# A one-core recurrence, Fourier mixing and MLP kernel: where the MLP pieces go, and what is kept in fixed order

## The chip, the core and the metric

The kernel runs on one core of a Trainium2 chip. The metric is the device time of one execution in microseconds (us). Before the change it is 781.95 us, the median of three runs (781.27 to 782.10); the profiled execution spans 780.2 us, and all times inside the trace are counted from its start.

## The reference, cut to what matters

Four batches, eight heads, 768 time steps, head size 48. First a delta-rule recurrence with a 48 x 48 state per batch and head, then, on its output put together to 768 x 384 per batch, a Fourier mixing, a normalisation and a two-layer MLP.

```python
# attention block: q, k, v are (4, 8, 768, 48), beta is (4, 8, 768)
k_n = k / (norm(k) + 1e-6)
for t in range(768):
    y[:, :, t] = einsum('bhd,bhde->bhe', q[:, :, t], state)
    v_old = einsum('bhde,bhd->bhe', state, k_n[:, :, t])
    state = state + beta_t * einsum('bhd,bhe->bhde', k_n[:, :, t], v[:, :, t] - v_old)

# x is y as (4, 768, 384)
mixed = real(fft(fft(x, axis=1), axis=2))
u  = x + mixed
un = (u - mean(u)) / sqrt(var(u) + 1e-6)                 # over the 384
out = u + maximum(un @ w_ch1, 0) @ w_ch2                  # 384 -> 1536 -> 384
```

The two weights arrive in 64-bit floating point and are turned into 32-bit on the core.

## The kernel before

**The recurrence in chunks.** Time is cut into chunks of 64 steps, 12 to a batch, so the chain has 48 steps m = 0 to 47. Each step needs the state of the step before it. It has three sections, each a group of small matmuls and then one operation of VectorE or ScalarE:

```python
def chain(m):
    ...                                   # pk = state x keys
    dve.tensor_tensor(U, V4[:, c], pk, op=ALU.subtract)      # section 0
    yield
    ...                                   # pu = wt x U
    act.activation(U, pu, ACT.Copy)                          # section 1
    yield
    ...                                   # pS = keys x U
    dve.tensor_tensor(nst, st, pS, op=ALU.add)               # section 2: the new state
    if n % 2 == 1:
        later.append(outputs(b, n, *pair))                   # y of two chunks, done later
    if c == QT - 1:
        scaled(Q + 1)                                        # V of the next four chunks x lengths
    yield
```

Four chunks make a quad Q, two quads a group g. Before its steps can run, a group needs `ahead(g)`: the keys and queries are transposed and their Gram matrices copied out of the matmul's memory (`prepare`), a triangular system is inverted on VectorE in 30 dependent rounds (`invert`), and the halves are put together by small matmuls and copies (`merge`). Groups 0 and 1 are prepared before the first chain step or during the first batch's steps.

```python
def gram_out(Q, c2, dst, src):
    if Q < 6 and c2:
        dve.tensor_copy(dst, src)
    else:
        act.activation(dst, src, ACT.Copy)

def invert(*gs):                          # per round j
    dve.tensor_tensor(t, X[:, :, j:j + 1, j + 1:], X[:, :, 0:j, j:j + 1], op=ALU.mult)
    dve.tensor_tensor(X[:, :, 0:j, j + 1:], X[:, :, 0:j, j + 1:], t, op=ALU.add)
    yield
```

**The mixing and the MLP.** When the chain of a batch has ended and its outputs are written to `x`, `fourier(b)` mixes it: sums and differences of halves on VectorE (`folded`, `shifted`), matmuls `pf` and `pb` with tables, additions back into `x`, and the statistics of the normalisation. For batch 0 the sums are made tile by tile (T = 2, 1, 0), since the last tile needs the last outputs. `mlps()` then works through the pairs of 128-row tiles, three pairs to a batch. Between two of its `yield`s lies a **piece**: mostly six matmul instructions `ph` (first layer) with one ScalarE operation, or four matmul instructions `po` (second layer).

**How they are laced together.** Python generators are advanced in turn. `beside()` advances the mixing of the last batch by one step, if there is one, and the MLP by one piece. `PRE` and `SIDE[b]` are the numbers of `ahead` steps and of pieces per section of a chain step, for the batch b whose chain is running.

```python
PRE, SIDE = 2.4, (0.0, 1.5, 2.2, 1.8)
pre, due, started = ahead(2), [0.0, 0.0], False
for m in range(NCH, STEPS):               # m = 12 .. 47
    b, n = divmod(m, NCH)
    g, Q = m // (2 * QT), m // QT
    count = 0
    while Q not in merged:                # the quad's merge is not traced yet
        advance(pre)
        count += 1
        if count % 3 == 0 and b > 1 or count % 4 == 0 and len(converted) == KF:
            beside()
    if m % (2 * QT) == 1:
        run(pre)
        pre = ahead(g + 1) if g + 1 < NG else iter(())
        due = [0.0, 0.0]
    for i, _ in enumerate(chain(m)):
        if i < 2:
            advancing(later)
        if n == 0 and i == 1:
            run(*later)
            later.clear()
            if b == 1:
                while advance(first_mixing):
                    if (0, 0) in norms or started:
                        started = advance(channels, 2)
            else:
                mixing[0] = fourier(b - 1)
        if b == 1 and (n > 0 or i > 1):
            advance(second, 3)            # second weight to 32 bit
        if m > NCH or i > 0:
            due[0] += 4.6 if g == 1 else PRE
            due[1] += SIDE[b]
        while max(due) >= 1.0:
            ...                           # beside() and advance(pre), one per unit due
run(*later)
mixing[0] = fourier(B - 1)
while beside() or mixing[0] is not None:
    pass
```

**Order.** The order of instructions on each engine is settled when the program is built: a scheduler may move an instruction ahead of others traced before it. While `strict[0]` is true, each TensorE, ScalarE and VectorE instruction is tied behind the one traced before it on its engine. That holds for the first batch's chain (m = 0 to 11) and a few places after it. What is traced later without this tie may still be moved in between.

```python
for m in range(1, NCH):                   # m = 1 .. 11, strict
    for i, _ in enumerate(chain(m)):
        ...                               # outputs, Gram matrices, merges at fixed places
        advance(next_keys, key_work.get((m, i), 0))
        if i == 1:
            ...
            elif m == 8:
                run(masks(2))
                advance(rest, 1)
            else:
                advance(rest, 5)          # first weight to 32 bit, then masks(3)
        if i == 2:
            advance(rest, 1)
            ...
            if m in (10, 11):
                advance(first_mixing)     # tiles 2 and 1 of the first mixing's sums
run(rest)
second = second_weight()
advance(second)
strict[0] = False
```

Of the kernel before, what the change touches and what calls it, by code (L numbers as in the profile page):

```python
# [82 lines left out]
def kernel(  # L83
# [15 lines left out]
    NCH = S // CH  # L99
# [3 lines left out]
    KF = DFF // 128  # L103
# [119 lines left out]
    def scaled(Q):  # L223

        if Q in vals and Q in lengths:
            vf = vals[Q].rearrange("p c u d -> p (c u) d")
            ln = lengths.pop(Q)
            dve.tensor_tensor(vf, vf, ln[:, :, None].broadcast_to([128, QT * 4, D]), op=ALU.mult)
# [129 lines left out]
    def second_weight():  # L358
        if moe_w_ch1.dtype == F32:
            yield  # L360
            nc.sync.dma_start(out=w2, in_=moe_w_ch2.rearrange("(c p) m -> p c m", p=128))
            converted.update(range(KF))
            return
        w2v = moe_w_ch2.bitcast(I32).rearrange("(c p) (m two) -> p c m two", p=128, two=2)

        stages = [xpairs[i].rearrange("p t (f two) -> p (t f) two", two=2).bitcast(I32) for i in (4, 5, 6)]

        def fetched(p):
            if p < KF:
                nc.sync.dma_start(out=stages[p % 3], in_=w2v[:, p])  # L370

        for p in range(3):
            fetched(p)
        yield
        digits(stages[0], *words(stages[0]))
        for p in range(KF):
            if p + 1 < KF:
                digits(stages[(p + 1) % 3], *words(stages[(p + 1) % 3]))
            ops = joined(w2[:, p], *words(stages[p % 3]))
            ops[0]()  # L380
            yield
            ops[1]()
            ops[2]()
            fetched(p + 3)
            converted.add(p)
            yield
# [3 lines left out]
    grams = {}  # L390

    def gram_out(Q, c2, dst, src):
        if Q < 6 and c2:
            dve.tensor_copy(dst, src)
        else:
            act.activation(dst, src, ACT.Copy)
# [8 lines left out]
    def masks(*Qs):  # L405

        for Q in Qs:
            for c2 in range(QT // 2):
                dst = ce(held[Q][2][:, 2 * c2:2 * c2 + 2])
                mask(Q, c2, dst, dst)  # L410
                yield

    def prepare(Q, parts=(0, 1)):
# [20 lines left out]
        for c2 in range(QT // 2):  # L434
# [29 lines left out]
            if 0 in parts:  # L464

                cj = slice(2 * QT * lh + 4 * c2, 2 * QT * lh + 4 * c2 + 4)
                Ae = A.rearrange("p l c (j e) s -> p e (c j) l s", e=2)[:, :, cj]
                for e in range(2):
                    gram_out(Q, c2, Ae[:, e], pv[:, e, :, 0, None, 0:W].broadcast_to([128, 4, 2, W]))
                for hh in range(2):  # L470
                    pr = slice(64 * hh + W, 64 * hh + 64)
                    gram_out(Q, c2, Ae[pr, :, :, 0], pv[pr, :, :, 0, W:])
# [172 lines left out]
    later = []  # L645
# [108 lines left out]
    def advancing(gens):  # L754

        if gens and next(gens[0], "end") == "end":
            gens.pop(0)
# [140 lines left out]
    done, converted = set(), set()  # L898
# [69 lines left out]
    def advance(gen, n=1):  # L968
        for _ in range(n):
            if next(gen, "end") == "end":  # L970
                return False
        return True

    def run(*gens):
        for gen in gens:
            for _ in gen:
                pass

    def seq(*gens):
        for gen in gens:  # L980
            yield from gen
# [74 lines left out]
    rest = seq(w.join(), masks(3))  # L1056
    first_mixing = fourier(0)
    for m in range(1, NCH):
        if m == 3:
            merges.update({2: Merge(1, 0, crossed=False), 3: Merge(1, 1, crossed=False)})  # L1060
        for i, _ in enumerate(chain(m)):
            if pe_work[m][i]:
                pe_work[m][i]()
            if m == 2 and i > 0:
                outs()
            if (m, i) in act_work:
                act_work[m, i]()
            advance(next_keys, key_work.get((m, i), 0))
            if i == 1:
                if m == 1:  # L1070
                    run(masks(0))
                    advance(first)
                elif m == 2:
                    scaled(1)
                    advance(first)
                elif m == 3:
                    run(masks(1))
                elif m == 6:
                    scaled(2)
                    advance(rest, 2)  # L1080
                elif m == 8:
                    run(masks(2))
                    advance(rest, 1)
                else:
                    advance(rest, 5)
            if i == 2:
                advance(rest, 1)
                if m in (3, 7):
                    w.split(10 + m // 7)
                if m in (10, 11):  # L1090
                    advance(first_mixing)
    run(rest)
    second = second_weight()
    advance(second)

# [12 lines left out]
    def ahead(g):  # L1108
        if g == 2:
            yield from kept(queries(4, 5))  # L1110
        for Q in (2 * g, 2 * g + 1):
            while Q >= NB and Q - NB in held and g > 2:
                yield
            if g > 2:
                yield from prepare(Q)
        yield from invert(g)
        for _ in merge(g):
            yield
# [4 lines left out]
    def beside():  # L1123

        if mixing[0] is not None:
            if not advance(mixing[0]):
                mixing[0] = None
        return advance(channels)


    PRE, SIDE = 2.4, (0.0, 1.5, 2.2, 1.8)
    pre, due, started = ahead(2), [0.0, 0.0], False
    for m in range(NCH, STEPS):
        b, n = divmod(m, NCH)
        g, Q = m // (2 * QT), m // QT

        count = 0
        while Q not in merged:
            advance(pre)
            count += 1  # L1140
            if count % 3 == 0 and b > 1 or count % 4 == 0 and len(converted) == KF:
                beside()
        if m % (2 * QT) == 1:
            run(pre)
# [15 lines that stand above are left out]
                advance(second, 3)  # L1160
# [4 lines that stand above are left out]
                if due[1] >= 1.0:  # L1165
                    due[1] -= 1.0
                    beside()
                if due[0] >= 1.0:
                    due[0] -= 1.0
                    advance(pre)  # L1170
# [34 lines left out]
```

## Time and profile before

| what | value |
|---|---|
| time, median of 3 | 781.95 us |
| profiled span | 780.2 us |
| TensorE (matmul) busy | 685.0 us, 88% |
| VectorE busy | 394.6 us, 51% |
| ScalarE busy | 258.1 us, 33% |
| GpSimd busy | 83.9 us, 11% |
| mean granted TensorE clock | 0.971 of full speed |
| mean DMA rate | 39 GB/s |

PE is TensorE's matmuls and PEld its weight loads, DVE is VectorE, ACT ScalarE, POOL GpSimd. Busy shares are means over parts of the program with different limits, so they say little about any one part; the table of stretches, which gives each engine's busy time, the granted clock and the DMA share between two given times, says more. The timeline of single instructions shows when one group of matmuls or one copy ran, and for how long.

The chain's sections can be found by their ScalarE operation `U<-pc`: step 0 at 89.8 us, step 12 (second batch) at 155.2, step 24 at 327.4, step 36 at 503.8, step 47 at 629.4. The last 100 us hold nothing but MLP.

### The profile page before, as it was taken

Reading aid. Unit: us, or ns where it says so; the run is one execution under the profiler, and the core shown is the slowest. Engines: PE = TensorE matmul, PEld = TensorE weight load, DVE = VectorE, ACT = ScalarE, POOL = GpSimd, SP = SyncE. Lnnn points to the kernel's source line nnn. Section 1 sums busy time; section 2 is a strip of 40 time slices with the busy share of each in tenths; the row PEclk is TensorE's granted clock in tenths of the full one; section 3 lists DMA queues with packets and bytes.
Section 4 is the critical chain, followed back from the end, with each engine's and each line's share of the span. In section 5 each row is a group of like instructions: output and inputs, shape, how many; then the busy total and the mean of one; then the engine's idle time right before and its main releaser. Section 6 shows DMA issues by size and latency. Waiting matters only on the chain.

```text
span 780.2 us, 18288 instructions
## 1 busy us (share of the span) xinstructions
PE 685.0 (88%) x7768; PEld 491.6 (63%) x7768; DVE 394.6 (51%) x980; ACT 258.1 (33%) x700; POOL 83.9 (11%) x116
## 2 busy tenths in 40 slices
PE   5943588869989998999899999878999989899996
PEld 4522577757747756567667577466667567577683
DVE  2599775977991399246595112887511125300000
ACT  3741355442335503535303444021623022021120
POOL 8010033323000000001100000011000000100000
PEclk9999999987999999999999999998999999999999
DMA  8642032341221211002201110100100000000000
GB/s 183 163 108 45 8 86 60 87 139 46 39 45 27 48 36 30 14 21 42 42 16 27 32 26 7 32 11 1 22 22 2 12 11 1 20 1 21 10 11 20
DMA packets 81041, 30.78 MB, mean 39 GB/s; under 512 B 75856, under 2 KB 77392, under 8 KB 80960
## 3 DMA queue, kind: packets, MB, share of 16 engines
q1 hardware_dynamic: 76560, 21.92, 13.2%
q0 software_dynamic: 2224, 7.31, 2.9%
q8 instruction: 61, 1.00, 0.5%
q10 hardware_dynamic: 2176, 0.39, 0.3%
q14 instruction: 20, 0.16, 0.1%
HBM read 24.87 MB, written 4.72 MB: 38 GB/s over the span
## 4 chain that ended last, share of the span: by engine, by line
PE 54%; DVE 26%; ACT 6%; SPq 5%; DMA 4%; issue 3%; POOL 1%; POOLq 0%; DVEq 0%; ACTq 0%
PE ph L131 20%; PE po L131 16%; DVE A L131 6%; DVE X L131 5%; PE pc L131 4%; SPq L219 4%; DVE x L131 3%; PE pf L131 3%; DVE w L131 3%; PE pj L131 2%; PE pb L131 2%; ACT A L131 2%; DMA qp<-in_q_dram 2%; ACT wt L131 2%; PE pg L131 2%
## 5 line engine op out<-in xcount | busy, mean ns | idle before, releaser
L131 PE MATMUL ph<-unT,w 128*128 128x256 f32 x864 | 212.1, 394 | 5.4 <-ACT hT L131 3.7
L131 PE MATMUL po<-w,hT 128*128 128x384 f32 x576 | 209.6, 508 | 0.0
L131 PEld LDWEIGHTS ph<-unT,w 128*128 128x128 f32 x864 | 159.8, 193 | 34.4 <-ACT hT L131 8.2
L131 PEld LDWEIGHTS po<-w,hT 128*128 128x128 f32 x576 | 105.6, 193 | 63.9 <-issue 4.9
L131 ACT ACTIVATE hT<-ph 128x256 f32<-128x256 f32 x144 | 55.0, 382 | 186.7 <-PE ph L131 186.3
L131 DVE TENSOR_TENSOR x<-x,po 128x384 f32<-128x384 f32 x24 | 13.2, 549 | 107.5 <-PE po L131 107.5
L131 PE MATMUL pg<-KQT 48*64 48x64 f32 (+1 forms) x1152 | 44.4, 297 | 5.8 <-ACT KQT L131 4.3
L131 ACT ACTIVATE U<-pc 128x192 f32<-128x192 f32 x48 | 15.8, 330 | 96.4 <-PE pc L131 82.7
L131 PEld LDWEIGHTS pg<-KQT 48*64 48x64 f32 x1152 | 34.0, 178 | 21.0 <-ACT KQT L131 11.0
L770 POOL DMA_INDIRECT out_dram<-x,rows_hi x12 | 12.3, 1025 | 321.1 <-DVE x L131 198.3
L131 DVE TENSOR_TENSOR U<-V,pc 128x192 f32<-128x192 f32 x48 | 16.7, 348 | 54.3 <-PE pc L131 54.3
L131 DVE TENSOR_TENSOR X<-X,A 128x30 f32<-128x30 f32 (+14 forms) x120 | 41.3, 344 | 3.0
L131 ACT ACTIVATE KQT<-pt 128x256 f32<-128x256 f32 (+1 forms) x84 | 33.0, 413 | 28.3 <-PE pt L131 26.9
L131 DVE TENSOR_TENSOR A<-X 128x30 f32<-128x30 f32 (+14 forms) x120 | 40.7, 339 | 3.0
L131 DVE TENSOR_TENSOR x<-x,pb 128x191 f32<-128x191 f32 (+1 forms) x72 | 24.9, 414 | 21.7 <-PE pb L131 21.7
L131 DVE TENSOR_TENSOR st<-st,pc 128x192 f32<-128x192 f32 x44 | 15.4, 350 | 40.2 <-PE pc L131 33.2
L131 PEld LDWEIGHTS pc<-U,wt 64*64 64x64 f32 x768 | 19.4, 156 | 24.2 <-DVE U L131 10.8
L131 PEld LDWEIGHTS pc<-st,KQT 48*64 48x64 f32 x768 | 18.6, 155 | 24.8 <-DVE st L131 11.9
L131 ACT ACTIVATE A<-pj 32x128 f32<-32x128 f32 (+1 forms) x76 | 20.7, 273 | 39.2 <-PE pj L131 38.4
L131 PE MATMUL pt<-pack,qp 128*128 128x128 f32 x96 | 22.4, 331 | 12.3 <-DMA qp<-in_q_dram 11.7
L131 PE MATMUL pc<-U,wt 64*64 64x48 f32 x768 | 25.8, 251 | 8.0 <-DVE U L131 6.2
L131 PE MATMUL pc<-st,KQT 48*64 48x48 f32 x768 | 25.3, 250 | 8.4 <-DVE st L131 8.1
(135 smaller groups left out, 855.3 us busy)
## 6 DMA issues: line engine op xcount, KB each, us to landing
x<-in_moe_w_ch_dram SPq DMA_DIRECT2D x14, 384.0 KB, 3.5
qp<-in_q_dram SPq DMA_DIRECT2D x96, 48.0 KB, 2.5
kp<-in_k_dram SPq DMA_DIRECT2D x80, 48.0 KB, 2.4
V<-in_v_dram SPq DMA_DIRECT2D x56, 48.0 KB, 2.3
w<-in_moe_w_ch_dram POOLq DMA_DIRECT2D x6, 384.0 KB, 8.2
x<-in_moe_w_ch_dram POOLq DMA_DIRECT2D x4, 384.0 KB, 7.7
V<-in_v_dram SPq DMA_DIRECT2D x64, 24.0 KB, 2.2
out_dram<-x SPq DMA_DIRECT2D x8, 192.0 KB, 1.9
```

Of the source, the lines that this page charges most:

```text
L131: ins = getattr(self.engine, name)(*args, **kwargs)
L219: eng.dma_start(out=vals[Q][64 * p:64 * p + CH, cs, u, :], in_=v[b, 4 * (p ^ (u % 2)) + u, t0:t0 + w * CH, :].rearrange("(c p) d -> p c d" ...
L770: nc.gpsimd.indirect_dma_start(out=out.rearrange("b s m -> (b s) m"), out_offset=bass.IndirectOffsetOnAxis(ap=rows_hi[:, i:i + 1], axis=0) ...
```

## The change

Five edits, none of which changes what is computed:

- the Gram matrices of quads 4 and 5 are copied out by ScalarE alone; before, VectorE took the second half of each;
- in step 11, the scaling of V for quad 3 is traced one section earlier, and at most three instead of five steps of the rest follow it;
- the last outputs of batch 0, and one more step of its mixing (sums of tile 0), are traced before the fixed order ends, so they keep their place;
- fewer MLP pieces beside the chain: 1.3 instead of 1.5 per section in batch 1, 2.0 instead of 2.2 in batch 2;
- more MLP pieces with the merges that a quad has to wait for: in batch 1 a piece after every step instead of every fourth, in the later batches after every second instead of every third or fourth.

The purpose is to have TensorE work at hand where it waits, and to have the first batch's end issued in the order in which its data become ready.

```diff
     def gram_out(Q, c2, dst, src):
-        if Q < 6 and c2:
+        if Q < 4 and c2:
             dve.tensor_copy(dst, src)
 ...
                 elif m == 8:
                     run(masks(2))
                     advance(rest, 1)
+                elif m == NCH - 1:
+                    scaled(3)
+                    advance(rest, 3)
                 else:
                     advance(rest, 5)
 ...
-    run(rest)
+    run(rest, *later)
+    later.clear()
+    advance(first_mixing)
     second = second_weight()
     advance(second)
 ...
-    PRE, SIDE = 2.4, (0.0, 1.5, 2.2, 1.8)
+    PRE, SIDE = 2.4, (0.0, 1.3, 2.0, 1.8)
 ...
             advance(pre)
             count += 1
-            if count % 3 == 0 and b > 1 or count % 4 == 0 and len(converted) == KF:
+            if len(converted) == KF and (b == 1 or count % 2 == 0):
                 beside()
```

## The prediction, made before the changed kernel was run

> **What bounds the kernel now.** I read the page's first two parts first, then a table of stretches, then single matmuls in the timeline. The page:
>
> ```profile
> PE 685.0 (88%) x7768; PEld 491.6 (63%) x7768; DVE 394.6 (51%) x980; ACT 258.1 (33%) x700; POOL 83.9 (11%) x116
> ...
> PE   5943588869989998999899999878999989899996
> DVE  2599775977991399246595112887511125300000
> ...
> PEclk9999999987999999999999999998999999999999
> ```
>
> TensorE is the busiest engine overall, and in the slices of 19.5 us it falls below 9 where VectorE rises to 7 to 9: in the first 200 us, and around 280, 390 and 490 to 550 us. So the bound changes from stretch to stretch. I cut the span at the ends of the inversions and mixings (columns: busy time and instructions of PE, PEld, DVE, ACT, POOL; granted clock; DMA share; GB/s):
>
> ```profile
> 104.00:152.00 48.00, 41.14 (x956) 34.75 (x956) 36.22 (x81) 26.20 (x69) 18.13 (x24) 1.00 0.36 86
> 152.00:176.00 24.00, 15.88 (x197) 13.75 (x196) 19.46 (x55) 10.05 (x22) 5.32 (x8) 0.85 0.41 120
> 176.00:236.00 60.00, 56.33 (x534) 38.56 (x533) 50.58 (x136) 19.29 (x55) 9.42 (x10) 0.90 0.19 42
> 236.00:270.00 34.00, 33.80 (x543) 26.20 (x542) 5.56 (x12) 20.16 (x58) 1.13 (x1) 0.98 0.19 37
> 270.00:312.00 42.00, 37.57 (x462) 24.46 (x454) 39.13 (x105) 9.07 (x25) 2.28 (x2) 1.00 0.18 36
> 312.00:378.00 66.00, 63.38 (x735) 44.80 (x736) 27.13 (x74) 30.07 (x86) 5.38 (x9) 1.00 0.14 28
> 378.00:420.00 42.00, 38.36 (x412) 25.61 (x411) 38.95 (x103) 9.68 (x27) 3.36 (x2) 1.00 0.12 27
> 420.00:484.00 64.00, 63.40 (x790) 45.00 (x790) 10.31 (x23) 28.63 (x88) 0.98 (x1) 1.00 0.11 23
> 484.00:556.00 72.00, 61.38 (x634) 43.20 (x625) 60.16 (x165) 17.60 (x45) 7.44 (x10) 0.91 0.08 18
> 556.00:636.00 80.00, 79.06 (x1008) 54.28 (x1008) 12.08 (x29) 21.52 (x65) 2.03 (x2) 1.00 0.03 12
> ```
>
> Length minus the first busy figure is TensorE's idle time: 6.9, 8.1, 3.7, 0.2, 4.4, 2.6, 3.6, 0.6, 10.6 and 0.9 us. Between them (236 to 270, 312 to 378, 420 to 484, 556 to 636, and the tail) TensorE has almost nothing to give. Its work is the same after the change, so the time can only fall where it stands still or runs slowly: above all 152 to 176 and 484 to 556, both mixings. What is missing in the second is seen if one asks for `po` alone:
>
> ```profile
> 322.00:367.00 45.00, 15.37 (x40) 6.79 (x40) 1.07 (x2) 1.00 0.12 26
> 498.70:543.70 45.00, 6.73 (x14) 3.08 (x14) 0.54 (x1) 0.85 0.04 12
> ```
>
> These are equal lengths from the first state of batch 2 and of batch 3, each holding a mixing. In the first TensorE does 40 `po` and 17 `ph` instructions beside it, in the second 14 and 32 (at the tail's pace of 0.325 and 0.216 us, 16.7 against 11.5 us of work). From 508.7 to 531 us there is no `po` and one `ph`: the MLP has used up batch 1 and waits for batch 2's statistics.
>
> The slow clock in that gap can be measured, too. One mixing matmul `pf` by one, from the timeline:
>
> ```profile
> 333.43 2.27 PE L131 MATMUL pf<-stab,scr 128*128 128x128 f32 x20
> 510.08 4.34 PE L131 MATMUL pf<-stab,scr 128*128 128x65 f32 x24 [2.38 <-DVE scr L131]
> ```
>
> 0.11 us each while MLP fills the gaps, 0.18 us each in the starved stretch.
>
> **What the Trainium skill says.** Its page "TensorE: Matmul & The Clock Gate", section "Part 1: The HAM clock gate (the "warmup" mystery)", says that TensorE's clock is halved after an idle window and freed again by sustained activity. The trace agrees in kind: the granted clock is 1.00 at 322 to 367 and 0.85 in the starved 498.7 to 543.7, and the `pf` above nearly double. It isn't consistent everywhere: from 40 to 80 us TensorE is mostly idle and the column still says 1.00. The page "Perfetto Trace Analysis", section "Engine Utilization", says that in a well-tuned kernel at least one engine approaches full utilisation; in the table above this holds except at 152 to 176, where VectorE has 19.5 of 24 us and TensorE 15.9.
>
> **The change part by part.**
>
> *Gram copies to ScalarE.* For each of quads 4 and 5, VectorE loses two copies of 128 x 256 (0.38 each) and two of 32 x 256 (0.43 each), as in
>
> ```profile
> 134.31 0.76 DVE L131 COPY A<-pg 128x256 f32<-128x256 f32 x2
> ...
> 135.96 0.86 DVE L131 COPY A<-pg 32x256 f32<-32x256 f32 x2
> ```
>
> 1.62 us a quad, 3.24 us in all. ScalarE gets them at the same kind of price (0.33 + 0.33 + 0.38 + 0.38 = 1.42 us, from its copies at 147.65 and 148.75), and is busy 26 of 48 us there. The first set sits before a merge matmul that waited 2.33 us for it; the second stands ahead of the sums of the mixing's tile 1 (153.47). Estimate on the path: 2 us of the 3.24.
>
> *Scaling of V in step 11.* Counting the advances, the rest's 36 + 2 steps are used up by step 10, so five or three makes no difference, and the scaling (0.95 us) already ran in step 11. 0 us.
>
> *Last outputs and tile 0 in order.* The y addition of the last outputs ran at 155.07, the first `pf` at 157.48; between them stand one section of chain step 12 and tile 0's sums. Nothing disappears, but conversion of the second weight and step 12 can no longer come in between so easily. The outputs' matmuls end at 153.0, ScalarE takes 0.49, the addition 0.55, the sums about 2: `pf` could start near 156. Estimate: 2 us with what the shorter wait saves behind it.
>
> *Pieces with the merges.* Batch 1, at step 16: by then 11 sections x 4.6 = 50 of the 58 steps that the first merged quad needs are done, so 8 are forced, and pieces with them go from 2 to 8. At 220 to 240 us TensorE is busy 17.0 of 20. Estimate: 2 of these 3 us. For batches 2 and 3 the old rule (every third or every fourth) hits 6 of 12 counts, the new one also 6 of 12: the rate is unchanged, 0 us.
>
> *Fewer pieces beside the chain.* Batch 1: 34 sections x 0.2 = 7 fewer, which the 6 above give back. Batch 2: 36 x 0.2 = 7 fewer, with nothing in return. A piece is 6 x 0.216 or 4 x 0.325 = 1.3 us, so 9.4 us of TensorE work leave the steps 24 to 35 and stay in store for the mixing of batch 2, which has 13 steps and takes a piece with each. The work isn't saved; it moves from where TensorE is full into the hole at 508.7 to 531, which has 6.3 us of idle time and a clock of 0.84 (0.16 x 22.3 = 3.6 us). From these 9.9 us I take 60%, as the mixing's own waits and VectorE (18.5 of 22.3 us busy) remain: 6 us. Against it, a third of the 7 pieces leave the inversions at 270 to 312 and 378 to 420, where VectorE sets the pace (39 of 42 us) and a missing piece becomes idle time: 7/3 x 1.3 = 3 us, of which some is refilled; I subtract 2. Net 4 us.
>
> Sum: 2 + 0 + 2 + 2 + 4 = 10 us, 781.95 - 10 = **772 us**.
>
> **The rivals.** *VectorE keeps the pace through both holes.* In 484 to 556 it is busy 60.2 of 72 us, and the inversion of the last group (from about 487 to 548) is a chain of dependent rounds. If the mixing and this inversion set that stretch's length, the moved pieces cost nothing there and the stretches that they left get shorter, so the gain survives. If instead pieces in TensorE's fixed queue hold up the mixing's matmuls, and so VectorE, the hole moves rather than fills: 2 to 5 us are left of my 10, some 778 us. For it speaks that the filled mixing at 322 to 367 took as long as the starved one; against it, that it did 5 us more MLP work and other preparation in that time.
>
> *The scheduler reshuffles.* Everything after step 12 without a tie may be placed anew, so parts that I hold to be unchanged can win or lose several us: 765 to 785 us. Nothing in the profile speaks against it.
>
> *The early part is bound by VectorE alone.* It is busy 70 of 84 us from 152 to 236. Then only the 3.24 us of copies count and the order gives nothing: 774 to 776 us.
>
> *The clock stays up.* Beyond the hole's 3.6 us, a TensorE that doesn't stand still from 160 to 190 (granted 0.82, 0.60 and 0.73 in its thirds) would save another 5 us or so: about 765 us. The change puts little new work there, so I give it a small weight.
>
> **Range and chances.** The large terms are bounded: idle time in the stretches that the change touches is 8.1 + 3.7 + 4.4 + 3.6 + 10.6 = 30 us, and I count on a third. 8 times in 10 I expect 762 to 782: the lower end is twice my sum, the upper end no gain at all. Faster by over 2% means below 766.3, which needs the clock or lucky order on top: 0.21. Slower by over 2% (above 797.6) would take a lost overlap as large as the biggest hole: 0.03. The rest, 0.76, is within 2%.
>
> **What the new profile would show.** Copies `A<-pg` on VectorE down from 16 to 8. The first `pf` a few us after step 11's outputs, earlier than 157.5. More pieces at the merge of step 16 and less idle time there. Chain steps 24 to 35 closer together. In batch 2's mixing, MLP matmuls all through, clock near 1.00, `pf` back at 0.11 us. A tail after the last mixing no longer than now. It would be wrong if the MLP still runs dry before batch 2's statistics, if inversions gain as much idle time as the mixing loses, or if the stretch 152 to 236 is as long as before.

## The result and the profile after

The changed kernel takes 776.06 us against 781.87 us before on the same chip (medians): ratio 0.9928, 95% interval 0.9910 to 0.9946. The profiled span falls from 780.2 to 773.7 us, 6.5 us. The prediction was 772 us in a range of 762 to 782.

The page of the changed kernel, busy time and the 40 slices:

```profile
PE 679.0 (88%) x7768; PEld 487.8 (63%) x7768; DVE 391.7 (51%) x972; ACT 261.4 (34%) x708; POOL 83.3 (11%) x116
...
PE   5934598779989989899998999899999989899996
DVE  2599776877980299336597122989311125300000
...
PEclk9999999877999999999999999899999989999999
```

TensorE's instructions are the same 7768. VectorE has eight fewer and ScalarE eight more: the Gram copies. The row PE shows where the time went only faintly, so here are the stretches of the changed kernel (busy time and instructions of PE, PEld, DVE, ACT, POOL; granted clock; DMA share; GB/s):

```profile
152.00:176.00 24.00, 16.72 (x199) 13.86 (x200) 19.32 (x58) 10.00 (x22) 5.95 (x8) 0.71 0.35 102
176.00:236.00 60.00, 55.70 (x497) 38.92 (x497) 48.43 (x126) 20.38 (x58) 9.82 (x11) 0.95 0.23 52
...
312.00:378.00 66.00, 60.48 (x681) 41.48 (x682) 26.85 (x74) 27.86 (x81) 5.39 (x9) 0.95 0.13 26
...
420.00:478.00 58.00, 56.96 (x740) 40.62 (x743) 10.41 (x23) 27.69 (x85) 0.98 (x1) 1.00 0.11 24
478.00:550.00 72.00, 65.99 (x709) 46.43 (x699) 60.53 (x165) 20.73 (x57) 6.98 (x10) 0.95 0.08 18
```

The stretch of 72 us around batch 2's mixing, which had 61.4 us of TensorE work, now has 66.0 and a clock of 0.95 instead of 0.91. I count it from 478 instead of 484, because the inversion in it begins 5.6 us earlier, at 480.8 instead of 486.4; the TensorE-bound stretch ahead of it is shorter by as much. In 312 to 378 TensorE's idle time has gone up, from 2.6 to 5.5 us, and at 152 to 176 the granted clock has fallen from 0.85 to 0.71 (from 176 to 236 it has risen from 0.90 to 0.95).

`po` alone, in the 45 us from the first state of batch 3, and the `pf` of that mixing:

```profile
493.10:538.10 45.00, 14.44 (x34) 6.59 (x34) 1.07 (x2) 0.93 0.04 12
```

```profile
502.92 2.28 PE L131 MATMUL pf<-stab,scr 128*128 128x65 f32 x20 [0.98 <-DVE scr L131]
```

34 `po` instead of 14 lie in the mixing, and a `pf` takes 0.11 us instead of 0.18. The hole was filled, as predicted.

**A ledger that takes the moved work out.** Pieces were moved about, so a chain step that comes earlier may just have had less MLP beside it. I therefore subtract from the time of each chain step's `U<-pc` the MLP work done by then (number of `ph` x 0.2157 us + number of `po` x 0.3256 us, the tail's pace). What is left may only grow where something else is done, or where TensorE waits or runs slowly. Growth in us between chain steps, from the profiles (rows add up to within 1.5 us of the span less all MLP work):

```
                    start to 16   16 to 24   24 to 36   36 to 40   40 to end
before                 206.9        37.0       75.2       38.8       47.7
after                  202.9        39.1       77.6       31.7       47.6
early_only             203.3        37.4       74.9       42.2       47.3
merge_side1            201.9        39.2       80.2       40.6       47.8
side2_back             202.8        37.6       80.2       38.6       46.0
side2_only             205.9        37.4       75.9       29.5       45.7
side2_only18           209.1        37.5       78.8       30.9       45.5
held_back              206.8        37.4       72.0       40.5       44.4
early_side2            204.0        37.4       76.6       29.9       44.4
no_merge_pieces        204.3        38.6       74.7       33.1       46.7
side1_back             201.9        40.1       79.5       31.7       47.6
```

The first two rows: the changed kernel is 4.0 us ahead at step 16, loses 2.1 by step 24 and 2.4 by step 36, and wins 7.1 in the mixing of batch 2 (steps 36 to 40). The net gain is that mixing's; the early gain is given back. The experiments ask whether that is so. The ledger tells where; how much is told by the timed runs, since a profile is one execution. That of the kernel before took 781.95 us, while its medians beside the experiments are 782.5 to 786.1; those of `side2_back` and `side1_back` lie 6.1 and 4.7 us under their medians, that of `side2_only18` 2.9 us above.

The theory is the **store**: MLP work of batch 1 held back until batch 2's mixing, where VectorE sets the pace and TensorE stood idle. The rivals: the gain is the fixed order at the end of batch 0 and the lighter VectorE (**order**), or chance in what the scheduler does (**luck**).

### The profile page after: what moved, and what is told of

It reads as the page before. It is cut to its first block, busy times and chain, and to the rows that moved or that the text cites. A ratio compares the mean times of both kernels' runs of the same rounds, so it can differ in the third digit from the quotient of the medians.

```text
span 773.7 us, 18281 instructions
## 1 busy us (share of the span) xinstructions
PE 679.0 (88%) x7768; PEld 487.8 (63%) x7768; DVE 391.7 (51%) x972; ACT 261.4 (34%) x708; POOL 83.3 (11%) x116
## 4 chain that ended last, share of the span: by engine, by line
PE 54%; DVE 14%; ACT 4%; issue 2%; DMA 1%; SPq 1%; POOL 1%; POOLq 0%; DVEq 0%; ACTq 0%
PE ph L131 20%; PE po L131 18%; DVE X L131 4%; PE pc L131 3%; DVE A L131 3%; PE pf L131 2%; PE pb L131 2%; DVE x L131 2%; ACT wt L131 2%; PE pg L131 2%; PE pt L131 2%; PE py L131 2%; ACT A L131 1%; PE ptr L131 1%; PE pj L131 1%
## 5 line engine op out<-in xcount | busy, mean ns | idle before, releaser
L131 PE MATMUL pt<-pack,qp 128*128 128x128 f32 x96 | 22.5, 331 | 13.9 <-DMA qp<-in_q_dram 13.1
```

Of the source, the lines that this page charges most:

```text
L131: ins = getattr(self.engine, name)(*args, **kwargs)
```

## The experiments

### The one number alone, and all but it

`side2_only`, on the kernel before:

```diff
-    PRE, SIDE = 2.4, (0.0, 1.5, 2.2, 1.8)
+    PRE, SIDE = 2.4, (0.0, 1.5, 2.0, 1.8)
```

> Only 2.0 instead of 2.2 pieces per section in batch 2, all else as before. Store theory (the gain is the MLP work kept for the mixing of batch 2, which had run dry): ratio 0.990 to 0.994, 774 to 777 us, with MLP matmuls between the start of batch 3 and its statistics. Rival, order: the gain came from the fixed order at the end of batch 0 and the lighter VectorE, so this alone gives within 2 us of before. Rival, scheduler's luck: anything from 770 to 790 us, without the hole being smaller.

Measured: 771.03 us against 786.09 before on that chip, ratio 0.9813 (0.9788 to 0.9838). I had expected 0.990 to 0.994: the gain is more than twice that.

`side2_back`, on the changed kernel:

```diff
-    PRE, SIDE = 2.4, (0.0, 1.3, 2.0, 1.8)
+    PRE, SIDE = 2.4, (0.0, 1.3, 2.2, 1.8)
```

> The changed kernel with 2.2 pieces per section in batch 2 as before. Store theory: the hole in the mixing of batch 2 is back, and 5 to 7 us of the 6 are lost, 780 to 783 us. Order rival: 776 us as in the changed kernel, as all of the early edits are in it.

Measured: 787.57 us, ratio 1.0015 (0.9998 to 1.0032). The one number gives more than the whole change, and without it the change gives nothing. The order rival falls, and luck becomes unlikely: the same number moves both kernels the same way, by 1.9% and by 0.9%. How the number works is seen in two stretches of each kernel, from 420 us to the beginning of the last inversion (its transposition `X<-A`), and from there to its end (`Z<-Y`). Before:

```profile
420.00:486.40 66.40, 65.80 (x827) 46.37 (x828) 10.91 (x24) 30.04 (x92) 0.98 (x1) 1.00 0.11 22
486.40:548.30 61.90, 51.93 (x512) 36.46 (x513) 52.20 (x153) 10.41 (x24) 7.44 (x10) 0.89 0.07 16
```

With 2.0 pieces, `side2_only`:

```profile
420.00:479.00 59.00, 58.12 (x787) 41.43 (x786) 9.48 (x19) 28.39 (x86) 0.96 (x1) 1.00 0.12 24
479.00:536.90 57.90, 54.23 (x532) 37.69 (x533) 52.48 (x154) 11.32 (x27) 6.94 (x10) 0.94 0.08 17
```

In the first stretch TensorE has no free time in either kernel, so every piece less makes it shorter: it ends 7.4 us earlier. In the second VectorE does the same 52 us of work, and the stretch shrinks by 4.0 us although 29.0 instead of 23.4 us of MLP lie in it: TensorE's idle time falls from 10.0 to 3.7 us, and VectorE's own from 9.7 to 5.4. 7.4 + 4.0 = 11.4 us, and the spans differ by 11.1. The pieces moved from the time in which TensorE was full to the time in which it wasn't, and did not merely fit in there.

Why the second stretch shrinks is seen in what VectorE waits for in it (us in total, times, longest). Its waits for the mixing's own matmuls `pf`, `pb` and `pd`, before:

```profile
DVE x L131 <- PE pb L131: 4.1, 2, 2.9
...
DVE scr L131 <- PE pf L131: 1.6, 2, 1.0
...
DVE x L131 <- PE pd L131: 0.5, 1, 0.5
```

and in `side2_only`, where this is the only one left:

```profile
DVE x L131 <- PE pb L131: 0.9, 1, 0.9
```

6.2 us have become 0.9, more than the 4.0 us by which the stretch is shorter. A `pf` took 0.18 us before and takes 0.11 us here:

```profile
501.84 2.40 PE L131 MATMUL pf<-stab,scr 128*128 128x64 f32 x22
```

Faster matmuls and another order on TensorE came together; no run separates them.

### The other parts alone

`early_only`, on the kernel before (Gram copies, scaling, last outputs and tile 0 in order):

```diff
-        if Q < 6 and c2:
+        if Q < 4 and c2:
...
+                elif m == NCH - 1:
+                    scaled(3)
+                    advance(rest, 3)
...
-    run(rest)
+    run(rest, *later)
+    later.clear()
+    advance(first_mixing)
```

> Only the three early edits: Gram copies on ScalarE, scaling in step 11, last outputs and tile 0 in fixed order. Store theory: steps 13 to 16 come 2 to 4 us earlier for the same MLP work, but the MLP then runs dry in batch 2's mixing as before, so 778 to 782 us. Order rival: 775 to 777 us.

Measured: 783.21 us against 786.09, ratio 0.9970 (0.9953 to 0.9987). 152 to 236 us, before and then `early_only`:

```profile
152.00:236.00 84.00, 72.21 (x730) 52.31 (x728) 70.04 (x189) 29.34 (x77) 14.74 (x18) 0.88 0.26 64
```

```profile
152.00:236.00 84.00, 72.59 (x779) 51.92 (x775) 67.91 (x183) 31.28 (x85) 15.73 (x18) 0.92 0.27 64
```

VectorE has 2.1 us less to do and TensorE gets 49 more instructions done in the same 84 us. By the ledger that is 3.6 us at step 16. In the dry mixing 3.4 us of it are lost again (42.2 against 38.8): an earlier chain only arrives earlier where work is missing. About 2.4 us by the timed ratio are left. The order changed by more than what was tied: the inversion in this stretch begins at 151.8 instead of 160.8 us and ends at 223.2 instead of 225.3. It begins at 151 to 152 in every kernel with the early edits and at 161 to 162 in every one without them.

`merge_side1`, on the kernel before:

```diff
-            if count % 3 == 0 and b > 1 or count % 4 == 0 and len(converted) == KF:
+            if len(converted) == KF and (b == 1 or count % 2 == 0):
...
-    PRE, SIDE = 2.4, (0.0, 1.5, 2.2, 1.8)
+    PRE, SIDE = 2.4, (0.0, 1.3, 2.2, 1.8)
```

> Only the pieces with the merges and 1.3 instead of 1.5 in batch 1. Store theory: the same number of pieces in batch 1, in another place; 1 to 2 us from the merge at step 16, then dry in batch 2's mixing: 779 to 782 us. My prediction's term for it was 2 us. Luck rival: 770 to 790 us.

Measured: 786.61 us, ratio 1.0013 (0.9996 to 1.0030): nothing. The ledger has 5.0 us of gain at step 16, and 2.2 + 5.0 us of loss to step 36.

### Is it the store at the start, or the rate?

`held_back`, the kernel before with 2.2 pieces, but none beside step 35:

```diff
                 if due[1] >= 1.0:
                     due[1] -= 1.0
-                    beside()
+                    if m != 35:
+                        beside()
```

> The kernel before, with its 2.2 pieces per section, except that in chain step 35, the last before batch 3, no piece is run beside the chain (6 to 7 pieces stay in store). Store theory: what counts is the store at the start of batch 3's mixing, not the rate before; as side2_only, 770 to 775 us. Rival, rate: the lower rate makes all of batch 2's steps shorter and only that counts; then one step without pieces gives 1 us or nothing, 784 to 787 us on this chip.

Measured: 777.84 us against 785.98, ratio 0.9908 (0.9883 to 0.9933). Both expectations miss: it is half of what `side2_only` gives. The same two stretches:

```profile
420.00:486.80 66.80, 65.97 (x843) 46.41 (x842) 11.27 (x25) 30.45 (x93) 0.98 (x1) 1.00 0.11 22
```

```profile
486.80:545.00 58.20, 50.98 (x502) 35.78 (x495) 50.52 (x153) 9.87 (x24) 6.83 (x10) 0.88 0.08 17
```

The first stretch is as long as before: step 35 begins at 476 us, so little was taken from where TensorE is full. The inversion holds no more MLP than before (22.5 us), only later in it, and is still 3.7 us shorter. But it isn't shorter for the reason seen in `side2_only`. TensorE waits longer ahead of the first `pf` than before (3.56 us against 2.38), the 24 of them run at 0.22 us each, and VectorE still waits for the mixing's matmuls, 6.4 us against 6.2:

```profile
500.79 5.19 PE L131 MATMUL pf<-stab,scr 128*128 128x65 f32 x24 [3.56 <-DVE scr L131]
```

```profile
DVE x L131 <- PE pb L131: 3.9, 2, 2.2
...
DVE x L131 <- PE pd L131: 1.9, 1, 1.9
DVE scr L131 <- PE pf L131: 0.6, 1, 0.6
```

Of the 3.7 us, 1.7 are VectorE's busy time (50.5 against 52.2 us for the same 153 instructions, closer packed) and 2.0 its other waits; why is open. So the gain of `side2_only` has two halves, the TensorE-bound stretch made shorter and the VectorE-bound one made shorter, and `held_back` shows that work kept from one step alone gives neither of them in the same way.

`side2_only18`, the kernel before with still fewer pieces:

```diff
-    PRE, SIDE = 2.4, (0.0, 1.5, 2.2, 1.8)
+    PRE, SIDE = 2.4, (0.0, 1.5, 1.8, 1.8)
```

> The kernel before with 1.8 pieces per section in batch 2: the store at the start of the mixing is about 18 us instead of 10 with 2.0 and 1 with 2.2. Store theory: the rest of the hole is filled, 0 to 4 us below side2_only, and no more. Rival, rate: as many us again as from 2.2 to 2.0, some 757 us. Rival, luck: no order among 2.2, 2.0, 1.8.

Measured: 775.31 us, ratio 0.9879 (0.9823 to 0.9934), by the medians 4 us above `side2_only`, where I expected 0 to 4 below; the intervals overlap by a little.

```profile
420.00:474.60 54.60, 53.85 (x737) 38.29 (x738) 11.12 (x25) 26.88 (x82) 2.03 (x2) 1.00 0.13 29
474.60:535.00 60.40, 55.48 (x513) 38.57 (x515) 50.35 (x149) 9.81 (x25) 5.78 (x9) 0.92 0.06 13
```

The first stretch falls again, but the second takes in only 29.6 us of MLP, 0.6 more than with 2.0, and gets longer. What it couldn't hold, 9 us, stands after it: from the end of the inversion to the end of the program it takes 241.5 us, against 232.2 with 2.0. The rival rate, with 757 us, is out. That 2.0 is better than 1.8 is what the medians and the stretches suggest, and isn't shown: the profile is of the slowest of the four runs, and on the changed kernel (next) 1.8 is no slower. Between 1.8 and 2.2 I only tried 2.0.

`side2_18` is the same on the changed kernel:

```diff
-    PRE, SIDE = 2.4, (0.0, 1.3, 2.0, 1.8)
+    PRE, SIDE = 2.4, (0.0, 1.3, 1.8, 1.8)
```

> The changed kernel with 1.8 instead of 2.0 in batch 2. Store theory: 0 to 4 us below the changed kernel, as it has 8.7 us in store at step 36 and the mixing takes up to 17: 772 to 776 us where the kernel before takes 782.

Measured: 774.34 us against 785.98, ratio 0.9879 (0.9822 to 0.9936). Its interval overlaps the changed kernel's, so whether it gains is open.

### Why the whole change gives less than its one number

`early_side2`, the edits of `early_only` and, in batch 2 alone:

```diff
-    PRE, SIDE = 2.4, (0.0, 1.5, 2.2, 1.8)
+    PRE, SIDE = 2.4, (0.0, 1.5, 2.0, 1.8)
```

> Early edits together with 2.0 pieces in batch 2, without the edits on the merges and on batch 1. By stretches, early_only was 3 us ahead at step 36 and gave it back in the dry mixing; with the store the 3 us should stay: 767 to 769 us. Rival: the early lead is lost elsewhere, 771 us or more.

Measured: 770.24 us against 785.98, ratio 0.9828 (0.9773 to 0.9884), by its median 1 to 3 us above what I expected. Its profile spans 767.0 us, 2.1 below `side2_only`, but by the ratios the two can't be told apart.

The last four kernels ran together, beside a kernel before of 782.45 us. It took 785.98 us on the same chip beside the four kernels ahead of them, so times are compared within each group of four, and across groups only the ratios. `after_again` is the changed kernel, without an edit:

> The changed kernel itself, on the chip of the three others, to compare them with it: 774 to 780 us, ratio to before 0.990 to 0.994.

Measured: 775.84 us, ratio 0.9929 (0.9902 to 0.9957). `early_side2_again` is `early_side2`, without an edit:

> Early edits with 2.0 in batch 2 and nothing else, on the same chip as the changed kernel: 4 to 7 us below it, if what the stretches say of the two other edits holds; 0 to 2 us below it, if their cost was an accident of one profile.

Measured: 770.09 us, ratio 0.9856 (0.9826 to 0.9886). The intervals don't meet: the changed kernel is slower by 5.8 us than the same kernel without the edits on the merges and on batch 1. So these cost time. `side1_back` has the merge pieces without the lower number in batch 1, on the changed kernel:

```diff
-    PRE, SIDE = 2.4, (0.0, 1.3, 2.0, 1.8)
+    PRE, SIDE = 2.4, (0.0, 1.5, 2.0, 1.8)
```

> The changed kernel with 1.5 pieces per section in batch 1 instead of 1.3, merge pieces as changed. Store theory: 6 to 7 pieces fewer in store when batch 1 is mixed, so the second mixing runs dry: 2 to 6 us above the changed kernel. Rival, nothing in it: the same within 2 us.

Measured: 781.91 us, ratio 0.9991 (0.9974 to 1.0008), 6 us above the changed kernel and 11.8 above `early_side2_again`, from which it differs in the merge pieces alone. They use up batch 0: at step 24 it has 2.2 us of MLP work left for the mixing of batch 1, `early_side2` 10.0. The 36 us from the first state of batch 2, all instructions and then `po` alone, first in `early_side2`:

```profile
319.70:355.70 36.00, 34.53 (x418) 23.16 (x409) 16.70 (x48) 13.42 (x39) 3.81 (x5) 1.00 0.13 28
...
319.70:355.70 36.00, 15.54 (x40) 6.71 (x40) 1.06 (x2) 1.00 0.13 28
```

and in `side1_back`:

```profile
325.70:361.70 36.00, 32.23 (x456) 23.22 (x457) 16.80 (x48) 13.24 (x39) 3.53 (x5) 0.86 0.12 26
...
325.70:361.70 36.00, 8.14 (x16) 3.22 (x16) 0.55 (x1) 0.86 0.12 26
```

16 `po` instead of 40 (and 2 `ph` instead of none), and a clock of 0.86: it is batch 2's hole once more, made in batch 1's mixing. In the ledger this hole (24 to 36) is 2.9 us; as much is lost from 16 to 24, and 3.2 us after step 40, so it is not the whole of the 11.8. The lower number in batch 1 repairs part of it (8.7 us left at step 24). `no_merge_pieces`, at last, is the changed kernel with the old rule for the merges:

```diff
-            if len(converted) == KF and (b == 1 or count % 2 == 0):
+            if count % 3 == 0 and b > 1 or count % 4 == 0 and len(converted) == KF:
```

> The changed kernel with the old rule for pieces with the merges; 1.3 and 2.0 beside the chain stay. If the merge pieces cost time (they use up store before the mixing of batch 1), this is 3 to 5 us below the changed kernel, near 770 us; it has 9 us more in store at step 24. If they are worth the 2 us I predicted, it is 2 us above it, 778 us.

Measured: 773.34 us, ratio 0.9881 (0.9846 to 0.9915). By the median 2.5 us below the changed kernel, but the intervals overlap. It has 16.3 us left at step 24, 7.6 more than the changed kernel and not the 9 that I wrote. By the median it is 3.3 us above `early_side2_again`, which had 10.0 left; these intervals overlap too, but nothing says that more in store is better without end.

## Why the prediction was right, and where its terms were not

The time lies in the range, 4 us above my number, and the mechanism for which I gave the largest term is the one that the runs show. That the sum came so near is luck: this term was more than twice as large alone as I put it, and another had the wrong sign. The terms themselves:

- *Gram copies and fixed order, 2 + 2 us.* The ledger has 3.6 us at step 16 with these edits alone, so the size was right there. Alone they bring 0.3% in the end, as the lead shrinks in the dry mixing. The inversion in the stretch 152 to 236 ends only 1.3 us earlier in the changed kernel (224.0 instead of 225.3), so by the length of this stretch alone, which I had named as a sign, they would have seemed to fail. VectorE's copies of `A<-pg` fell from 16 to 8; the first `pf` starts at 156.66 instead of 157.48.
- *Scaling in step 11, 0 us.* Not tried by itself. V's scaling still runs in step 11, at 145.79 instead of 147.10 us.
- *Fewer pieces in batch 2, net 4 us.* The failed step is the size. Alone it gave 11.1 us of span, and 1.9% of the time. I took 60% of the hole, 6 us; the inversion took in 5.6 us more MLP and was shorter by 4.0 on top, 9.6 together. I then took off 2 us for two inversions left short, at 270 to 312 and 378 to 420. The first of them doesn't belong here: batch 2's steps run from 327 to 504 us. The second grew from 35.3 to 35.9 us in `side2_only`, so the loss was 0.6 us.
- *Pieces with the merges, 2 us, and fewer in batch 1.* The failed step is the sign. The pieces came out of a limited store, and I had counted that store only for batch 2. That 6 more and 7 fewer pieces nearly balance was right (8.7 us of MLP left at step 24 against 10.0); that they bring 2 us was not, since the changed kernel is 5.8 us slower than the one without both.
- *The rivals.* VectorE does set the pace in the last inversion, and the moved work helps all the same, as the first rival's first half says. The second rival, the scheduler, is in part what happened: the inversion that began at 160.8 us moved ahead by 9 us with the early edits, which I hadn't foreseen. The third (the order gives nothing early) can't be ruled out: I had put the copies of both quads at 3.24 us, and the 3.6 us at step 16 are of copies and order together. The fourth, the clock, stayed out: 0.71 instead of 0.85 at 152 to 176, 0.95 instead of 0.90 after it.
- *A reading.* I wrote that one engine is near its limit in every stretch but 152 to 176. In 104 to 152 and 484 to 556 none is above 86%.

Of what the two edits cost, 5.8 us by the timed runs and 6.7 between the profiles, I can place a part: the changed kernel gains 1.1 us on `early_side2` up to step 16, loses 1.7 to step 24, 1.0 to step 36, 1.8 in batch 2's mixing and 3.2 after step 40. Of the last, 2.7 lie after step 47, in the last mixing and the tail; they have no explanation here.

Of all that was run, `early_side2` and `side2_only` are the fastest, with 770.1 to 771.0 us, faster than the kernel before; only `early_side2` was timed beside the changed kernel, and it is faster than that, too.

## What to carry to other kernels

Where one engine's filler work is run beside a chain, ask not how much filler a stage can take but how much is left for the stage that has nothing else. Here a filler that ran dry in a stage paced by another engine cost twice, in TensorE's idle time and in slower matmuls for which the other engine waited. Subtract the filler from the time of each step of the chain before comparing two schedules, or an earlier step says nothing. And time the parts of a bundle of edits one by one: here one number was worth more than all five edits together.

## What the runs showed that I had not expected

A VectorE-bound stretch became shorter when more TensorE work was put into it. `side2_only` shows it: 5.6 us more MLP lie in the last inversion, and it is 4.0 us shorter, as VectorE's waits for `pf`, `pb` and `pd` fall from 6.2 to 0.9 us. The Trainium skill's page "TensorE: Matmul & The Clock Gate", section "HAM oscillation — how this bites in real kernels", tells of idle gaps that slow the matmuls after them. Three runs agree: the first `pf` of this mixing came after a gap of 0.98 us in the changed kernel, 2.38 before and 3.56 in `held_back`, and the row that follows took 0.11, 0.18 and 0.22 us for each. Others don't fit the gap alone: in `no_merge_pieces` it is 0.89 us, and ten `pf` at 494.33 us take 0.23 us each. `side2_only` shows what it saves on the second engine when they are fast.

The column of the granted clock is a weaker witness than such a duration. In the kernel before it says 1.00 from 104 to 152 us, while the 16 matmuls `pc` of a chain step take 0.68 us there, as at 107.40, and 0.45 us later, as at 192.47:

```profile
107.40 0.68 PE L131 MATMUL pc<-st,KQT 48*64 48x48 f32 x16 [0.80 <-DVE st L131]
...
192.47 0.45 PE L131 MATMUL pc<-st,KQT 48*64 48x48 f32 x16
```

The kernels that run dry also vary more from run to run. On the chip of `side2_only` the kernel before took from 781.8 to 789.1 us and `side2_back` from 781.5 to 791.1, `side2_only` from 770.4 to 772.0, though with 4 runs against 48 and 20. That the dry stretches are the cause was not tried.
